# Attention and soft MoE on one core: the attention loop by pairs of heads instead of by heads

## The chip, the cores and the metric

The kernel runs on one core of a Trainium2 chip. The metric is the device time of one execution in microseconds (us). Before the change it took 432.06 us in the median of three runs (430.77 to 432.63).

The engines are named as in the profile: PE is TensorE (matmul; PEld its weight loads), DVE is VectorE, ACT is ScalarE, POOL is GpSimd, SP is the engine that issues nearly all DMAs.

## The reference

```python
# q, k, v: (8, 12, 448, 64); every head on its own, causal
scores = np.where(mask, -1e9, (q @ k.T) / 8)
attn = exp(scores - max(scores, -1)); attn /= attn.sum(-1) + 1e-9
x = (attn @ v) of all heads, as (3584, 768)        # 448 rows a batch, 12 heads x 64 columns
logits = x @ phi                                   # (3584, 32 slots)
d = softmax(logits over the 3584 rows)             # dispatch
slot_input = d.T @ x                               # (32, 768), 4 slots an expert
slot_out[e] = relu(slot_input[e] @ w1[e]) @ w2[e]  # 8 experts, 768 -> 1024 -> 768
out = softmax(logits over the 32 slots) @ slot_out # (3584, 768)
```

All is float32. w1 and w2 together are 50 MB, the largest input.

## The kernel before

There are 96 heads; the two heads of a pair p (48 pairs, six to a batch) share the loads and the casts. All transfers are DMAs of a pair: queries and keys q(p), k(p) of 448 KB each into three raw buffers in turn (the order is k(p), q(p), k(p+1), ...), and v with a column of ones, 260 KB, into two.

**One head i.** The scores lie transposed, keys on partitions, in one of three PSUM tiles `s` of two banks. They are made in two parts. `scores1` (lines 252 to 281, seven matmuls) adds the causal mask and rounded keys times rounded queries. `max_keys` (283 to 302) finds a maximum over groups of 32 keys on DVE (one long reduction of 128x1024, two short ones); `max_row` (304 to 313) transposes them on PE (tile `rt`) and reduces them on DVE (`mr`), and `max_spread` (315 to 324) writes them into rows of `r2` on POOL. `scores2` (326 to 335, four matmuls with `k2` and `r2`) adds what the rounding left out and takes the maxima away. `exps` is one ACT instruction over the tile; it frees the tile and leaves `pt`. `attv` (341 to 353) multiplies by v with 64 output columns at a time: stationary `pt`, moving 65 columns of v (the 65th is the sum), into the PSUM bank `po`. The 448 queries are four chunks, three of 128 and a last one of 64; chunk qc needs qc + 1 products for each 64 queries. `norm` (355 to 372) divides on DVE and writes `x`.

**Operands of a pair.** On ACT `cast_k` and `cast_q` round keys and queries (`ks`, `qd`), `copy_k2` fills `k2`; on POOL `sub_k` and `sub_q` form the rests (`ks` and `r2`). `ks`, `qd` and `r2` have two buffers, `k2` one. A raw buffer is free once its subtraction is done.

**Routing.** `xtrans` (377 to 383) transposes a pair's x on PE (tile `xt`, copied by ACT to `xts`). Three times a batch `next_logits` multiplies two pairs by phi (tile `g`, 32 output columns at a time); `logits_b`, `logits_d` and `logits_e` keep a running maximum and exponentials over the rows, and `dispatch` adds d.T @ x in two halves (tile `sp`, 32 output columns). `rt`, `xt`, `g`, `sp` and `tp` (of `logits_e`) share one PSUM bank, `misc`, with one buffer.

**The order.** Every engine keeps the order in which the program is written (`keep_in_program_order`). The loop of lines 525 to 582 goes by heads, and two lists (lines 48 to 53) give the order inside an even and an odd head; `plan` and `plan_a` (448 to 460) add routing at fixed heads.

```python
("ck", "mr0", "mr1", "sp", "sk", "c3", "c0", "k3", "c12", "k1", "k0", "k2", "t0", "t2", "t1", "t3", "exp", "pa",
 "x0", "plan", "x1", "x2", "cq", "a0", "a1", "a2", "a3", "n0", "n1", "n2", "ld"),
```

Here `c`, `k` are parts of scores1 of head i+2, `t` of scores2 of head i, `exp` its exp, `x` max_keys of i+2, `mr`, `sp` the maxima of i+1, and `a`, `n` products and norm of head i-1. `ck`, `sk`, `cq` work on pair p+2, as do `sq` in the odd list; `c2` is copy_k2 of p+1. On PE a head is thus: rt, scores1, scores2, xt or routing, products with v.

**After attention** the last head's rest of the path, then the experts and the output, for which w1 and w2 stream in; 23 of their 768 KB units are loaded during attention, one in every odd pair, and 12 buffers lie where attention's tiles were.

Of the kernel before, what the change touches and what calls it, by code (L numbers as in the profile page):

```python
# [9 lines left out]
F32 = mybir.dt.float32  # L10
# [7 lines left out]
P = 128  # L18
# [14 lines left out]
NR, XB, XT = 2, 3, 3  # L33
# [14 lines left out]
ORDER = (  # L48
# [4 lines left out]
)  # L53

SC0, SC1, SC2, SC3 = 576, 0, 320, 512
RW, RC, RF = 96, 4, 20
CQ0 = (0, 128, 256, 384)
# [29 lines left out]
def attention_soft_moe(ctx: ExitStack, tc: tile.TileContext, qk, va, phi, w1, w2, out):  # L87
# [17 lines left out]
    qd_, kf_ = [fix.tile([P, 2, S], F32R, name="qd0")], [fix.tile([P, 2 * S + KP], F32R, name="ks0")]  # L105
    x_[1] = fix.tile([P, NCH, 3 * P], F32, name="x1")
    qd_.append(fix.tile([P, 2, S], F32R, name="qd1"))
    zero = fix.tile([P, P // 2], F32, name="zero")
    r_ = [fix.tile([P, RW], F32, name=f"r{i}") for i in range(2)]
    kf_.append(fix.tile([P, 2 * S + KP], F32R, name="ks1"))  # L110
# [3 lines left out]
    kf_.append(fix.tile([P, 2 * S + KP], F32R, name="k2"))  # L114
    *ks_, k2_ = (k[:, 0:2 * S].rearrange("p (h s)->p h s", h=2) for k in kf_)
# [84 lines left out]
    pob = ps_1.tile([P, NCH * VC], F32, name="po")  # L200
    po0 = pob.rearrange("p (a b)->p a b", b=VC)
    identb = const.tile([P, P], BF16, name="identb")

    nc.vector.memset(zero, 0.0)
    nc.vector.tensor_copy(out=identb, in_=ident)
    for i in range(NR):
        nc.gpsimd.memset(r2_[i][0:64, :, :].bitcast(F32), 0.0)
        if i == 0:
            nc.vector.memset(k2_[0:64, :, :].bitcast(F32), 1.0)
    nc.vector.memset(pob, 0.0)  # L210
    for k in kf_:
        nc.vector.memset(k[:, 2 * S:2 * S + KP].bitcast(F32), 0.0)
    for i in range(2):
        nc.vector.memset(r_[i], -3.0e38)
# [12 lines left out]

    def cast_q(p, hs=slice(0, 2)):
        if p < NPAIR:
            nc.scalar.activation(out=qd_[p % NR][:, hs], in_=st["raw", 0, p][:, hs], func=AF.Copy)  # L230

    def cast_k(p, hs=slice(0, 2)):
        if p < NPAIR:
            nc.scalar.activation(out=ks_[p % NR][:, hs], in_=st["raw", 1, p][:, hs], func=AF.Copy)

    def sub_k(p, hs=slice(0, 2), eng=None):
        if p < NPAIR:
            ks = ks_[p % NR][64:P, hs]
            (eng or nc.gpsimd).tensor_tensor(out=ks, in0=st["raw", 1, p][64:P, hs], in1=ks, op=ALU.subtract)

    def copy_k2(p, hs=slice(0, 2)):
        if p < NPAIR:
            nc.scalar.activation(out=k2_[64:P, hs], in_=ks_[p % NR][0:64, hs],
                                 func=AF.Copy)
# [7 lines left out]
    def scores1(i, part):  # L252
# [3 lines left out]
        ks, qd = kf_[p % NR], qd_[p % NR]  # L256
# [69 lines left out]
    def scores2(i, cs):  # L326
# [4 lines left out]
        k2, r2 = kf_[NR], r2_[p % NR]  # L331
# [9 lines left out]
    def attv(i, qcs):  # L341
        if not 0 <= i < NHD:
            return
        p, h = divmod(i, 2)
        pt, v, po = pt_[i % 2], va_[p % 2], st.get(("po", i), po0)
        begun = st.setdefault(("begun", i, id(po)), set())
        for qc in qcs:
            for c in range(qc + 1):
                col = SCOL[c] + P * (qc - c)
                for u in range(0, P if qc < 3 or i == NHD - 1 and c == 3 else 64, AW):  # L350
                    nc.tensor.matmul(po[u:u + AW, qc], pt[:, col + u:col + u + AW], v[:, c, h],
                                     start=u not in begun, stop=c == qc, skip_group_check=True)
                    begun.add(u)

    def norm(i, k):
        if not 0 <= i < NHD:
            return
        p, h = divmod(i, 2)
        if k == 0:
            if i % 6 == 0:  # L360
                xn = x_[p // 3 % XB]
                st["xn", p // 3] = xn
                for k in range(3):
                    st["x", p + k] = xn[:, :, P * k:P * k + P]
            sm = st["sm", i] = moe.tile([P, NCH], F32, tag="sm", name=f"sm{i}", bufs=2)
            nc.vector.tensor_scalar(out=sm, in0=st.get(("po", i), po0)[:, :, HD], scalar1=EPS, scalar2=None, op0=ALU.add)
        elif k == 1:
            nc.vector.reciprocal(out=st["sm", i], in_=st["sm", i])
        else:
            sm = st.pop(("sm", i))  # L370
            nc.vector.tensor_tensor(out=st["x", p][:, :, HD * h:HD * h + HD], in0=st.get(("po", i), po0)[:, :, 0:HD],
                                    in1=sm.unsqueeze(2).to_broadcast([P, NCH, HD]), op=ALU.mult)

# [74 lines left out]
    plan, plan_a = {}, {}  # L448
    for b in range(NB):
        o, last = 12 * b, b == NB - 1  # L450
        for j in range(PPB if not last else PPB - 2):
            plan_a[o + 2 * j + 4] = lambda p=b * PPB + j: xtrans(p)
        for j, r in ((0, 9), (2, 11)):
            plan[o + r] = lambda b=b, j=j: next_logits(b, j, misc(f"g{b}_{j}"))
        if not last:
            plan[o + 15] = lambda b=b: (next_logits(b, 4, misc(f"g{b}_4")), logits_b(b, lt))
            plan_a[o + 17] = lambda b=b: logits_e(b)
            hs = ((19, (0,)), (25, (1,))) if b < NB - 2 else ((19, (0, 1)),)
            for r, hfs in hs:
                plan[o + r] = lambda b=b, hfs=hfs: [dispatch(b, hf) for hf in hfs]  # L460


    warm(START[0], a=zero.bitcast(BF16))
# [26 lines left out]
    scores1_all(2)  # L490
    warm(START[3])
# [4 lines left out]
    sub_q(1, h0)  # L496
# [27 lines left out]
    nload = 0  # L524
    for i in range(NHD):
        p, h = divmod(i, 2)
        if h:
            load_qk(p + 3, 1)
            if p + 1 < NPAIR - 1:
                loads_v(p + 1)  # L530
            load_qk(p + 3, 0)
            if p % 2 and nload < RES:
                load_w(nload)
                nload += 1
        if i == NHD - 3:

            loads_v(NPAIR - 1, nc.scalar)
        if i < 2:
            scores2(i, (1, 0, 2))
            if i:  # L540
                scores1_all(3)
            scores2(i, (3,))
            exps(i)
            if i == 0:
                max_row(1, 0)
                warm(START[4], pob[:, 0:P])
                max_row(1, 1)
                sub_k(1, h1, nc.vector)
                max_spread(1)
                sub_q(1, h1)  # L550

        for n in ORDER[h]:
            if i < 2 and (n == "exp" or n[0] in "kt" or n in ("c0", "c3", "c12")):
                continue
            if i == 0 and n in ("mr0", "mr1", "sp"):
                continue
            if n[0] == "k" or n in ("c0", "c3", "c12"):
                scores1(i + 2, n)
            elif n[0] == "t":
                scores2(i, (int(n[1]),))  # L560
            elif n[0] == "a":
# [336 lines left out]
```

## Time and profile before

| | |
|---|---|
| median of the runs | 432.06 us |
| profiled execution | 430.89 us, span 429.2 us |
| mean granted TensorE clock | 0.979 |
| busy: PE, PEld | 396.0, 317.6 us |
| busy: DVE, ACT, POOL | 297.6, 287.5, 266.2 us |
| DMA | 119.18 MB, mean 278 GB/s |

The page of the profile lists groups of equal instructions as line, engine, operation, out<-in and shape, with busy time, mean ns of one, and the idle time before them and what ended most of it. All instructions carry line L71, that of the helper that keeps the order, so one goes by tiles. For PE, "128*64" means 128 rows and 64 columns of the array. A matmul's end is modelled in the trace; the distance from start to start tells more. PE's instructions are twice the matmuls where the operands are plain float32: each of those is run in two. The timeline gives start, duration, engine, operation and tiles; consecutive equal instructions are merged into one row with their count.

### The profile page before, as it was taken

What the parts mean: (1) busy time and instruction counts of PE and PEld (TensorE: products, weight loads), DVE (VectorE), ACT (ScalarE), POOL (GpSimd) and SP (SyncE); (2) the same over time, 40 slices, a digit from 0 to 9 for tenths busy, and PEclk for the clock granted to TensorE, in tenths of its full rate; (3) what the DMA queues carried; (4) which work ended last, traced back from release to release, by engine and by line L of the source; (5) the groups of instructions that cost most, each with busy time, mean ns of one, the idle gap of its engine ahead of it and who ended that gap; (6) DMA issues with size and microseconds to landing.
All of it is one profiled execution on the core that took longest, in us unless ns stands there. A gap on an engine that the chain in (4) does not pass through costs nothing. (4 is left out here: it accounts for less than half of the span.)

```text
span 429.2 us, 14091 instructions
## 1 busy us (share of the span) xinstructions
PE 396.0 (92%) x5782; PEld 317.6 (74%) x5782; DVE 297.6 (69%) x861; ACT 287.5 (67%) x400; POOL 266.2 (62%) x216
## 2 busy tenths in 40 slices
PE   6898999999999999999999999999989998998740
PEld 3687888898898889888988888898868654544430
DVE  4687788778777877787787877778775477423440
ACT  5587879787887888887878788878865211333330
POOL 5799998888888788887887888888861000000000
PEclk8999999999999999999999999999999999999985
DMA  7476777777677776777776776677759999999997
GB/s 266 137 246 225 216 267 258 248 250 224 222 260 256 238 237 213 246 254 243 237 229 226 256 269 236 211 227 268 268 210 344 411 413 422 425 419 411 400 393 328
DMA packets 34481, 119.18 MB, mean 278 GB/s; under 512 B 3824, under 2 KB 8944, under 8 KB 32880
## 3 DMA queue, kind: packets, MB, share of 16 engines
q1 hardware_dynamic: 34272, 118.01, 77.5%
q8 instruction: 46, 0.75, 0.7%
q10 hardware_dynamic: 144, 0.27, 0.2%
q14 instruction: 19, 0.16, 0.1%
HBM read 107.25 MB, written 11.01 MB: 276 GB/s over the span
## 5 line engine op out<-in xcount | busy, mean ns | idle before, releaser
L71 ACT ACTIVATE pt<-s 128x1024 f32<-128x1024 f32 x96 | 98.2, 1023 | 57.2 <-PE s L71 51.8
L71 PEld LDWEIGHTS po<-va,pt 128*64 128x64 f32 x3040 | 117.8, 137 | 22.1 <-issue 21.6
L71 PE MATMUL po<-va,pt 128*64 128x65 f32 x3040 | 131.0, 225 | 0.0
L71 DVE TRANSPOSE_TENSOR_REDUCE r<-s 128x32 f32<-128x1024 f32 x96 | 118.2, 1231 | 2.4 <-PE s L71 2.0
L71 POOL TENSOR_TENSOR r<-qk,qd 64x896 fp32r<-64x896 f32 (+1 forms) x50 | 101.2, 2023 | 6.5 <-ACT qd L71 2.7
L71 POOL TENSOR_TENSOR ks<-qk,ks 64x896 fp32r<-64x896 f32 (+1 forms) x47 | 97.8, 2080 | 6.6 <-ACT ks L71 3.5
L71 POOL TENSOR_SCALAR_AFFINE_SELECT r<-mr 14x448 fp32r<-14x448 f32 x96 | 61.9, 645 | 47.5 <-DVE mr L71 43.4
L71 PE MATMUL s<-qd,ks 128*128 128x448 f32 (+3 forms) x384 | 76.5, 310 | 2.3 <-DVE ks L71 2.3
L71 PE MATMUL s<-r,k 128*128 128x320 f32 (+3 forms) x384 | 65.0, 290 | 3.5 <-ACT k L71 2.1
L71 PEld LDWEIGHTS s<-r,k 128*128 128x128 f32 (+1 forms) x384 | 54.3, 176 | 8.3 <-POOL r L71 5.6
L71 PEld LDWEIGHTS s<-qd,ks 128*128 128x128 f32 (+1 forms) x384 | 55.3, 182 | 3.1 <-DVE ks L71 2.5
L71 DVE TENSOR_SCALAR sm<-po 128x4 f32<-128x4 f32 x95 | 15.4, 162 | 52.9 <-PE po L71 51.8
L71 ACT ACTIVATE ks<-qk 128x896 fp32r<-128x896 f32 (+1 forms) x50 | 46.1, 923 | 8.1 <-DMA qk<-in_qk_dram 4.3
L71 ACT ACTIVATE qd<-qk 128x896 fp32r<-128x896 f32 (+1 forms) x50 | 46.1, 923 | 1.8 <-DMA qk<-in_qk_dram 1.7
L71 ACT ACTIVATE k<-ks 64x896 fp32r<-64x896 f32 (+1 forms) x49 | 45.8, 934 | 1.1
L71 DVE TENSOR_TENSOR x<-po,sm 128x256 f32<-128x256 f32 x95 | 40.3, 425 | 3.3
L71 PE MATMUL s<-tri,identb 128*128 128x64 bf16 (+2 forms) x288 | 39.6, 234 | 0.0
L71 PEld LDWEIGHTS <-identb 128*128 128x128 bf16 x339 | 35.0, 107 | 4.9 <-issue 3.1
L71 DVE TENSOR_REDUCE r<-r 128x16 f32<-128x32 f32 x192 | 34.1, 177 | 5.4
L71 PE MATMUL rt<-ident,r 128*76 128x128 f32 x96 | 28.8, 300 | 2.7 <-DVE sm L71 0.8
L71 PE MATMUL xt<-ident,x 128*128 128x128 f32 x188 | 29.7, 281 | 0.1
L71 DVE TENSOR_REDUCE mr<-rt 14x32 f32<-14x128 f32 x96 | 25.8, 269 | 3.8 <-PE rt L71 3.6
(136 smaller groups left out, 360.6 us busy)
## 6 DMA issues: line engine op xcount, KB each, us to landing
qk<-in_qk_dram SPq DMA_DIRECT2D x94, 448.0 KB, 4.0
w<-in_w_dram SPq DMA_DIRECT2D x43, 768.0 KB, 6.9
w<-in_w_dram SPq DMA_DIRECT2D x10, 1536.0 KB, 19.1
va<-in_va_dram SPq DMA_DIRECT2D x47, 260.0 KB, 3.2
out_dram<-ot SPq DMA_DIRECT2D x16, 384.0 KB, 6.7
out_dram<-ot SPq DMA_DIRECT2D x2, 1536.0 KB, 9.3
qk<-in_qk_dram SPq DMA_DIRECT2D x4, 224.0 KB, 3.4
hw<-in_w_dram SPq DMA_DIRECT2D x1, 768.0 KB, 6.4
```

The costliest lines, as they stand in the source:

```text
L71: return self._tc.keep_in_program_order(op(*args, **kwargs))
```

## The change

The loop goes by pairs: `block(p)` with heads a = 2p and a+1 replaces the lists and the plan. On PE its order is scores2(a), scores1(a+2), scores2(a+1), xt of pair p-1, scores1(a+3), all with the full width; then the products with v of head a, rt(a+2), the products of head a+1, the last query chunks of both heads side by side (`attv3`), rt(a+3), and last the routing product, if there is one. `po` holds both heads in one bank, as seven groups of 65 columns: three chunks of each head and one that has head a's last chunk in rows 0 to 63 and head a+1's in rows 64 to 127. The products of both heads stand in the block of their exps, and norm is done once for a pair. rt takes 64 columns instead of 76. sub_q works on pair p+1 instead of p+2, cast_k on p+3 instead of p+2. The transposed x has two buffers instead of three.

```diff
-NR, XB, XT = 2, 3, 3
+NR, XB, XT = 2, 3, 2
...
-            nc.tensor.transpose(out=st["rt", i][0:RW - RF, 0:P], in_=r_[i % 2][:, RF:RW], identity=ident)
+            nc.tensor.transpose(out=st["rt", i][0:AW, 0:P], in_=r_[i % 2][:, RF:RF + AW], identity=ident)
...
+    def attv3(p):
+
+        for c in range(NCH):
+            for h in range(2):
+                col = SCOL[c] + P * (NCH - 1 - c)
+                nc.tensor.matmul(po2[AW * h:AW * h + AW, NQ - 1], pt_[h][:, col:col + AW], va_[p % 2][:, c, h],
+                                 start=False, stop=c == NCH - 1, skip_group_check=True)
...
+    def block(p):
+        a, b = 2 * p, p // 6 - 1
+        last, m6 = p == NPAIR - 1, p % 6
+        begun = set()
+        if not last and p + 1 < NPAIR - 1:
+            loads_v(p + 1)
+        elif not last:
+            loads_v(p + 1, nc.scalar)
+        if p % 2 and p // 2 < RES:
+            load_w(p // 2)
+
+        scores2(a, range(NCH))
+        exps(a)
+        scores1_all(a + 2)
+        for k in range(3):
+            max_keys(a + 2, k)
+        scores2(a + 1, range(NCH))
+        if m6 == 2 and b >= 0 and p > 6:
+            logits_e(b)
+        if p:
+            xtrans(p - 1)
+        exps(a + 1)
+        scores1_all(a + 3)
+        max_keys(a + 3, 0)
+        sub_q(p + 1)
+        load_qk(p + 3, 1)
+        sub_k(p + 2)
+        load_qk(p + 3, 0)
+        if m6 == 1 and p > 6:
+            logits_d(b, lt)
+        copy_k2(p + 1)
+        cast_q(p + 2)
+        cast_k(p + 3)
...
+        attv(a, [(qc, qc, FULL) for qc in range(3)], po2, begun)
+        max_row(a + 2, 0)
+        attv(a + 1, [(qc, 3 + qc, FULL) for qc in range(3)], po2, begun)
+        max_row(a + 2, 1)
+        max_spread(a + 2)
+        for k in (1, 2):
+            max_keys(a + 3, k)
+        attv3(p)
+        norm(p, 0)
+        max_row(a + 3, 0)
+        max_row(a + 3, 1)
+        max_spread(a + 3)
+        for _ in range(2):
+            if later and p:
+                later.pop(0)()
+
+        if m6 in (3, 5) and p > 6:
+            sp = misc(f"sp{b}_{m6 // 5}")
+            dispatch_a(b, m6 // 5, sp)
+        for k in (1, 2):
+            norm(p, k)
+        if m6 in (3, 5) and p > 6:
+            dispatch_b(b, m6 // 5, sp)
+        if m6 in (2, 4) and p >= 2:
+            next_logits(p // 6, m6 - 2, misc(f"g{p}"))
+        elif m6 == 0 and p:
+            next_logits(b, 4, misc(f"g{p}"))
+            logits_b(b, lt)
+
+    for p in range(NPAIR):
+        block(p)
...
-                     dynamic_dma_scratch_size=1024)
+                     dynamic_dma_scratch_size=256)
```

`later` holds twelve one-off fills on POOL, now two in a block. Ahead of the loop, three memsets of x's last chunks on DVE and cast_k of pair 2 on ACT are added; the warm-up matmuls and scores1 of head 2 that stood between the first heads' steps go out or into block 0. In the last block head a's products stand alone, and the last head's path behind the loop stays as it was, without the xt of pair 46.

More of the change, by code (lines that the diff above doesn't have):

```diff
@@ L349, in attv @@
                 col = SCOL[c] + P * (qc - c)
[L350 to L358, printed above, removed]
-        if k == 0:
[L360 to L366, printed above, removed]
+                for u, w in us:
+                    if u and qc == NCH - 1 and c < qc:
+                        continue
+                    nc.tensor.matmul(po[w:w + AW, k], pt[:, col + u:col + u + AW], v[:, c, h],
+                                     start=w not in begun, stop=c == qc, skip_group_check=True)
+                    begun.add(w)
@@ L446, in dispatch @@
         dispatch_b(b, hf, sp)
[L448 to L463, printed above, removed]
+    warm(START[0], a=x_[1][:, NCH - 1, 0:AW].bitcast(BF16))
     h0, h1 = slice(0, 1), slice(1, 2)
```

162 lines of the change are left out of this document (67 added, 95 removed), and 4 rows, old and new, of the table ORDER.

## The prediction

> **What bounds the kernel now.** I read the page first, then the stretches, then one pair of heads in order of time. The page's engine line and costliest groups (busy, mean ns of one, idle time before and who ended it):
>
> ```profile
> PE 396.0 (92%) x5782; PEld 317.6 (74%) x5782; DVE 297.6 (69%) x861; ACT 287.5 (67%) x400; POOL 266.2 (62%) x216
> ...
> L71 PEld LDWEIGHTS po<-va,pt 128*64 128x64 f32 x3040 | 117.8, 137 | 22.1 <-issue 21.6
> ```
>
> The stretches, cut at every twelfth transposition of maxima (rt), are six pairs of heads each, one batch; first and last of six (us; busy us and count of PE, PEld, DVE, ACT, POOL; clock, DMA share, GB/s):
>
> ```profile
> 62.46:102.23 39.77, 39.37 (x619) 34.35 (x619) 31.52 (x91) 32.85 (x43) 33.02 (x25) 1.00 0.74 246
> 261.36:301.15 39.79, 39.39 (x620) 34.37 (x618) 31.50 (x91) 32.74 (x43) 32.90 (x25) 1.00 0.72 241
> ```
>
> A pair takes 39.78/6 = 6.63 us, TensorE has work in 99% of it, at granted clock 1.00, and DVE, ACT and POOL need 5.25, 5.46 and 5.48 us. So the order of work on TensorE sets the pace, but three engines stand within 1.4 us of it. TensorE over one head:
>
> ```profile
> 203.29 0.65 PE L71 MATMUL g<-xts,phi 128*32 128x128 f32 x16
> 203.86 1.38 PE L71 MATMUL po<-va,pt 128*64 128x65 f32 x32
> 205.17 0.30 PE L71 MATMUL rt<-ident,r 128*76 128x128 f32 x1
> 205.31 0.25 PE L71 MATMUL s<-tri,identb 128*128 128x64 bf16 x2
> 205.48 0.67 PE L71 MATMUL s<-qd,ks 128*128 128x320 f32 x3
> 205.99 0.68 PE L71 MATMUL s<-r,k 128*128 128x448 f32 x4
> 206.50 0.63 PE L71 MATMUL xt<-ident,x 128*128 128x128 f32 x4
> 207.06 0.28 PE L71 MATMUL po<-va,pt 128*64 128x65 f32 x2
> ```
>
> From start to start: first scores 0.68, second scores 0.51, x's transposition 0.56, products with v 1.31, a routing product g 0.57.
>
> **What the change takes off TensorE.** Two things. First the last query chunk. These are the weight loads of po up to a cut, and of a whole group:
>
> ```profile
> 210.36 0.77 PEld L71 LDWEIGHTS po<-va,pt 128*64 128x64 f32 x23 [0.20 <-issue]
> 203.86 1.24 PEld L71 LDWEIGHTS po<-va,pt 128*64 128x64 f32 x32 [0.20 <-issue]
> ```
>
> Less the 0.14 of one load, 23 loads start within 0.63 us, 29 ns apart; the other nine take 0.47 us, 52 ns each. The code says why: 12 products (24 loads) alternate between output rows 0-63 and 64-127, the last four (8 loads) have no partner. attv3 puts head 0 and head 1 side by side, so 16 loads a pair go from 52 to 29 ns: 16 x 0.023 = 0.37 us; with the first instruction after them, to 205.17, nearer 0.43. I take 0.40.
>
> Second, changes of tile width. po's loads sat idle 22.1 us ahead of 95 groups, 0.23 each, and 1.31 - 1.24 = 0.07 on the way out. One of two such groups a pair goes: 0.30. Nothing else leaves TensorE; the 32 products (64 loads) and both score parts stay. 6.63 - 0.70 = 5.93 us a pair if nothing else decides.
>
> **What it adds there.** The routing products (g, and sp of the dispatch) now stand right behind the second rt, and all three use the one scratch bank "misc". rt must be read by DVE (mr) first. rt takes 0.30, then mr 0.27 and two hand-offs of about 0.05: TensorE stands 0.55 us in five of six pairs, 0.46 on average. In before another head's work lies between. exps(a+1) moves behind the copy of xt on ACT, costed at 0.13 us in every other pair: a block (one pair, heads a and a+1) has second, first and second scores and xt, 0.51 + 0.68 + 0.51 + 0.47 = 2.17 us; with 0.2 until xt has ended, 0.5 for its copy and 1.05 for the exp, ACT is done at 3.92, and TensorE, after 0.68 first scores, 0.09 change of width, 0.74 products and 0.11 rt, is there at 3.79. (With 0.70 + 0.46 products and a second rt such a block, without routing, is 5.1 us.) Doing nothing there bounds it at 0, a whole exp late at 1.0. Two pairs: 11.86 + 0.92 + 0.13 = 12.9 us, against 13.26 now.
>
> **Moved steps and the chain they make.** Here is the danger. In before, sub_q(p+2) ran a pair ahead and key loads were issued straight behind it, so that cast_k had about 6.3 us from issue on:
>
> ```profile
> 197.08 2.10 POOL L71 TENSOR_TENSOR r<-qk,qd 64x896 fp32r<-64x896 f32 x1
> 199.21 0.33 SPq L71 DMA_DIRECT2D qk<-in_qk_dram  x1
> 206.37 0.64 POOL L71 TENSOR_SCALAR_AFFINE_SELECT r<-mr 14x448 fp32r<-14x448 f32 x1 [0.48 <-DVE mr L71]
> 207.09 2.11 POOL L71 TENSOR_TENSOR ks<-qk,ks 64x896 fp32r<-64x896 f32 x1
> 205.47 0.95 ACT L71 ACTIVATE ks<-qk 128x896 fp32r<-128x896 f32 x1
> 203.40 1.02 ACT L71 ACTIVATE pt<-s 128x1024 f32<-128x1024 f32 x1 [0.83 <-PE s L71]
> 202.74 0.27 DVE L71 TENSOR_REDUCE mr<-rt 14x32 f32<-14x128 f32 x1
> 202.93 1.23 DVE L71 TRANSPOSE_TENSOR_REDUCE r<-s 128x32 f32<-128x1024 f32 x1
> 200.99 0.40 DVE L71 TENSOR_REDUCE r<-r 128x16 f32<-128x32 f32 x2
> ```
>
> Over the whole run ACT waited for keys five times:
>
> ```profile
> ACT ks L71 <- DMA qk<-in_qk_dram: 4.3, 5, 1.4
> ```
>
> The three raw buffers turn over so that k(p+3) takes the one of q(p+1). In after, sub_q(p+1) is emitted in block p itself, behind both spreads of block p-1 on POOL, and cast_k(p+3) ends block p on ACT, with exps of the next block queued behind it. From the end of sub_q: issue 0.03, landing L, hand-off 0.07, cast 0.95, exp 1.02, hand-off 0.07 (2.14 + L); then the first scores of the second head, whose bank that exp frees, 0.84 to their end (205.31 to 205.48 + 0.67) and 0.03 to their reduction; 1.23, mr of the head before 0.20, two reductions 0.40, hand-off 0.05, rt 0.30; mr 0.10 + 0.27, hand-off 0.07, spread 0.64 + 0.08, sub_q 2.10 (6.31). That closes over two blocks: **two pairs take at least L + 8.45 us**. In the block with logits_e the scratch bank goes rt, tp, copies on ACT, xt, before those scores: some 1.2 us more, once in three hops.
>
> L is the unknown. Every other block issues a 768 KB weight load 2.4 to 3.0 us ahead of the keys, and only those blocks matter (a load alone gives 3.3 + 8.45 = 11.75, under 12.9). The DMA view, cut to single issues: keys at 185.84, 199.21, 212.42 and 238.99 behind a weight load; keys at 192.5 with a free queue; keys 3.7 us behind a weight load at 39.08; and the weight load at 314.98, which had only va 0.4 us ahead of it:
>
> ```profile
> qk<-in_qk_dram SPq DMA_DIRECT2D x1, 448.0 KB, 5.3
> qk<-in_qk_dram SPq DMA_DIRECT2D x1, 448.0 KB, 5.7
> qk<-in_qk_dram SPq DMA_DIRECT2D x1, 448.0 KB, 5.2
> qk<-in_qk_dram SPq DMA_DIRECT2D x1, 448.0 KB, 6.0
> qk<-in_qk_dram SPq DMA_DIRECT2D x1, 448.0 KB, 3.2
> qk<-in_qk_dram SPq DMA_DIRECT2D x1, 448.0 KB, 3.4
> w<-in_w_dram SPq DMA_DIRECT2D x1, 768.0 KB, 4.4
> ```
>
> In the four slow cases q (0.4 us) and va (1.1) had been issued just ahead of the weights. In after, SP issues va, weights, then keys some 2.9 us later, and q comes over 1.4 us ahead; that is nearest to the last row, where the weights had landed by 4.4. So L lies between 3.2 and 6.0; I take 3.6, near the free queue. The hops are then 12.9, 12.9 and 12.05 + 1.2 = 13.25: 39.05 a batch, 0.73 less than 39.78. Over some 40 pairs (6.67 batches): -4.9 us.
>
> POOL's own order (two subtractions, two spreads, four hand-offs: 2.10 x 2 + 0.64 x 2 + 0.3 = 5.8) is covered under 6.4 a pair. Norm over seven columns costs DVE about what it saves, and DVE has 1.4 us a pair to hide it. Two buffers for the transposed x cost nothing: g has read pairs p-2 and p-1 before xt(p) is written, a block later. The smaller DMA scratch costs nothing, as no issue in the rows is POOL's.
>
> **Start and end.** The first spread ends at 13.50; in after block 0 can begin there and reach rt of head 3 after its 5.1 us, at 18.6 against 20.21: -1.6. The three new memsets of x's last chunks (about 0.35 each, an estimate from the 0.81 of 896 columns below) stand on DVE before 4.05, where it had waited 0.87 for ACT: 0.2 is uncovered, and 1.05 if that cover goes. At the end, the row at 326.18 is the last rt and that at 331.75 the last head's products; the last row is the stretch of the first seven pairs:
>
> ```profile
> 12.86 0.64 POOL L71 TENSOR_SCALAR_AFFINE_SELECT r<-mr 14x448 fp32r<-14x448 f32 x1 [2.76 <-DVE r L71]
> 20.21 0.28 PE L71 MATMUL rt<-ident,r 128*76 128x128 f32 x1 [0.81 <-DVE sm L71]
> 326.18 0.30 PE L71 MATMUL rt<-ident,r 128*76 128x128 f32 x1
> 331.75 1.25 PEld L71 LDWEIGHTS e<-va,pt 128*64 128x64 f32 x34
> 333.86 0.60 PE L71 MATMUL xt<-ident,x 128*128 128x128 f32 x4
> 1.76 0.81 DVE L71 MEMSET k<- 64x896 f32 x1
> 4.05 0.62 DVE L71 TENSOR_TENSOR ks<-qk,ks 64x448 fp32r<-64x448 f32 x1 [0.87 <-ACT ks L71]
> 17.81:62.46 44.65, 42.01 (x663) 37.34 (x662) 34.70 (x97) 35.62 (x41) 41.92 (x41) 1.00 0.67 225
> ```
>
> After has one head less outstanding (rt + 1.2 of g + 3.7 = 4.9 against 5.6) and no xt in between: -1.3. The first seven pairs run at 6.38 us with POOL busy 94%, its one-off fills included; I expect 6.2 there: -1.2. The weight stream behind starts when attention frees its memory, so it moves along one for one. Sum: -4.9 - 1.6 - 1.3 - 1.2 = -9.0. The profiled execution took 430.89 (span 429.2), the median is 432.06; I count from the median: **423 us**.
>
> **Rivals.** (1) *The keys come late, slower.* If the queue behaves as in the four slow rows, L is 5.0 (half a microsecond off for the emptier queue): hops 13.45, 13.45, 14.65 = 41.55, +1.77 a batch, +11.8; the first seven pairs lose 7 x (6.73 - 6.38) = 2.4, start and end give 2.9: 443. At L = 5.5 a batch is 43.05: some 455. It decides from L about 4.5 on, where a batch takes 40.05 and the first pairs and that loss take back what start and end give. For it: four rows of the same distance; against: 3.4 and 4.4. (2) *TensorE's gain passes whole*, no chain, no bank wait: 5.93 a pair, 47 x 0.70 = -33: 399. It needs L below 3.4 and mr ready at once; ACT and POOL would then have work in 92% of a pair (5.46 and 5.48 of 5.93), which leaves little room for waits in their order. (3) *rt doesn't fit into the narrow stage*: it shrinks to 64 columns to stay there. If a transposition still takes the whole array, the group is left and entered twice more, 2 x 0.30 a pair: each hop 1.2 longer, 14.1, 14.1, 14.45, +2.9 a batch, +19, less 4 at start and end: 447. The trace has only full-width ones (128*76). The Trainium skill, "TensorEngine Tiling (Array Packing)", Restrictions and Gotchas, says that column tiling and transpose mode exclude each other for fp32 inputs; by that rule this rival holds. No run here shows it yet. (4) *Nothing to tell*: L near 4.5 eats the gain: 432.
>
> **How the numbers follow.** A measurement here tells no change to about 0.5%, 2.2 us. Forecast 0.48 (its own range 413 to 429), late keys 0.25, whole gain 0.08, wide rt 0.07, no difference 0.12. Faster: 0.48 + 0.08, less 0.02 that falls near the bound: 0.54; same 0.15; slower 0.31. The range leaves out the whole gain and the worst late keys: 410 to 445.
>
> **What would show it.** Right: loads of po 29 ns apart to the end of the group, half as many idle entries; ACT ks waiting for DMA qk in every other pair; g and sp of TensorE waiting for DVE mr. Wrong: no DMA wait ahead of ks (no chain, rival 2), or landings over 4.5 us in the blocks with weights (rival 1), or a gap on both sides of each rt (rival 3).

## The result, and the profile after

The changed kernel takes **451.7 us** in the median of four runs (449.92 to 452.62); the kernel before took 431.41 beside it (430.72 to 432.63). The ratio is 1.0462, with a 95% interval of 1.0419 to 1.0505: slower by 4.6%, where 423 us had been forecast, and outside the range of 410 to 445.

The page of the kernel after (engine line, chain by engine, loads of po):

```profile
PE 389.0 (86%) x5763; PEld 297.2 (66%) x5763; DVE 300.0 (67%) x817; ACT 288.5 (64%) x400; POOL 264.3 (59%) x215
...
PE 48%; DMA 20%; DVE 9%; issue 7%; POOL 6%; ACT 6%; SPq 0%; DVEq 0%; POOLq 0%; ACTq 0%
...
L65 PEld LDWEIGHTS po<-va,pt 128*64 128x64 f32 x3040 | 97.9, 139 | 17.9 <-issue 11.9
```

TensorE does work in 7 us less, in a span that is 20.7 us longer: it waits now, in 14% of the span instead of 8%. The loads of po save 20 us of busy time against 117.8 before, and their idle time with the releaser "issue" is down from 21.6 us in 89 places to 11.9 in 48, so the side-by-side stage and about half as many entries are there.

Stretches of the kernel after: the first seven pairs, then two of the six batches of twelve rt (us; busy and count of PE, PEld, DVE, ACT, POOL; clock, DMA share, GB/s), and the sum of all six:

```profile
15.73:64.75 49.02, 42.55 (x696) 35.99 (x693) 35.98 (x97) 36.47 (x43) 41.48 (x41) 1.00 0.68 220
...
143.25:187.55 44.30, 40.14 (x623) 33.23 (x619) 31.92 (x85) 32.84 (x43) 32.70 (x24) 0.96 0.68 216
...
230.63:272.11 41.48, 38.63 (x622) 31.90 (x619) 31.85 (x85) 32.61 (x43) 32.72 (x24) 1.00 0.70 227
...
sum 255.05, PE 233.75 PEld 192.68 DVE 191.14 ACT 197.65 POOL 196.53; mean PE 38.96 PEld 32.11 DVE 31.86 ACT 32.94 POOL 32.75
```

Six batches took 6 x 39.8 before; now they take 255.05. The quietest takes 41.48, so +1.7 a batch (10 us) is there always; the others add 6 us in all.

Where the 20.7 us of span are, from the starts of rt: up to rt of head 2 **-2.1** (15.73 against 17.81); the seven pairs behind it **+4.4** (49.02 against 44.65); from there to the last rt **+13.7** (277.4 against 263.7: six batches counted from that rt take 255.05 against 238.69, +16.4, and the pairs behind them 22.4 against 25.0, -2.7, since one of these took 8.9 before); from the last rt (342.18, before 326.18) to the end **+4.7** (107.7 against 103.0).

One pair with a g and without any late transfer takes 6.80 us instead of 6.50. First its stretch before and after, then TensorE over it in the kernel after:

```profile
205.17:211.67 6.50, 6.50 (x110) 5.84 (x109) 5.02 (x15) 5.28 (x7) 5.49 (x5) 1.00 0.58 178
```

```profile
201.84:208.64 6.80, 6.35 (x112) 5.40 (x108) 5.17 (x14) 5.27 (x7) 5.45 (x4) 1.00 0.82 277
```

```profile
201.84 0.30 PE L65 MATMUL rt<-ident,r 128*64 128x128 f32 x1
202.58 0.64 PE L65 MATMUL g<-xts,phi 128*32 128x128 f32 x16 [0.45 <-DVE mr L65]
203.15 0.74 PE L65 MATMUL s<-r,k 128*128 128x448 f32 x4
203.73 0.26 PE L65 MATMUL s<-tri,identb 128*128 128x128 bf16 x2
...
204.49 0.63 PE L65 MATMUL s<-r,k 128*128 128x448 f32 x4
204.96 0.63 PE L65 MATMUL xt<-ident,x 128*128 128x128 f32 x4
205.43 0.25 PE L65 MATMUL s<-tri,identb 128*128 128x128 bf16 x2
...
206.25 0.92 PE L65 MATMUL po<-va,pt 128*64 128x65 f32 x24
207.10 0.30 PE L65 MATMUL rt<-ident,r 128*64 128x128 f32 x1
207.33 1.39 PE L65 MATMUL po<-va,pt 128*64 128x65 f32 x40
208.64 0.30 PE L65 MATMUL rt<-ident,r 128*64 128x128 f32 x1
```

```profile
207.32 1.25 PEld L65 LDWEIGHTS po<-va,pt 128*64 128x64 f32 x40
```

From start to start, in us:

| part of a pair | before | after |
|---|---|---|
| products with v, with the rt of the first head | 1.31 + 0.14 + 1.31 = 2.76 | 0.85 + 0.23 + 1.31 = 2.39 |
| second rt up to the next instruction | 0.14 | 0.74 |
| first and second scores, xt | 3.03 | 3.10 |
| g | 0.57 | 0.57 |

The 40 loads of 207.32 stand 28 ns apart (1.25 less the 0.14 of one, over 39): side by side works to the end of the group. But of the 0.70 us that were to go only 0.37 went, and 0.60 came in at the scratch bank. That is +0.30 for a pair whose TensorE meets nothing else.

The waits of the kernel after (us in total, times, longest) that bear on this:

```profile
ACT ks L65 <- DMA qk<-in_qk_dram: 19.2, 20, 2.4
PEld g L65 <- DVE mr L65: 14.6, 23, 0.6
```

ACT's waits for keys went from five to twenty, 4.3 to 19.2 us, as the chain of the forecast says; but they are the smaller part of the loss. The landings that the forecast called the unknown: keys issued behind a weight load, from 63.39 to 318.16, took 3.2 to 6.0 us, 4.3 in the median, where 3.6 was taken. The four slowest of them (5.3 to 6.0) stand ahead of pairs of 7.6 to 9.7 us.

### The profile page after: what moved, and what is told of

Read it like the earlier page. It is cut to its first block, busy times and chain, and to the rows that moved or that the text cites. A ratio compares the mean times of both kernels' runs of the same rounds, so it can differ in the third digit from the quotient of the medians.

```text
span 449.9 us, 14022 instructions
## 1 busy us (share of the span) xinstructions
PE 389.0 (86%) x5763; PEld 297.2 (66%) x5763; DVE 300.0 (67%) x817; ACT 288.5 (64%) x400; POOL 264.3 (59%) x215
## 4 chain that ended last, share of the span: by engine, by line
PE 48%; DMA 20%; DVE 9%; issue 7%; POOL 6%; ACT 6%; SPq 0%; DVEq 0%; POOLq 0%; ACTq 0%
PE s L65 17%; PE po L65 16%; DMA w<-in_w_dram 14%; DMA qk<-in_qk_dram 7%; POOL r L65 5%; DVE r L65 4%; PE xt L65 4%; PE rt L65 3%; ACT pt L65 3%; PE sp L65 2%; PE g L65 2%; DVE mr L65 2%; PE pp L65 1%; PE hp L65 1%; POOL ks L65 1%
## 5 line engine op out<-in xcount | busy, mean ns | idle before, releaser
L65 PE MATMUL po<-va,pt 128*64 128x65 f32 x3040 | 111.1, 226 | 0.1
L65 PEld LDWEIGHTS po<-va,pt 128*64 128x64 f32 x3040 | 97.9, 139 | 17.9 <-issue 11.9
L65 PE MATMUL s<-qd,ks 128*66 128x64 f32 (+3 forms) x384 | 78.4, 315 | 2.6 <-DVE ks L65 1.9
L65 PEld LDWEIGHTS s<-r,k 128*128 128x128 f32 (+1 forms) x384 | 59.1, 175 | 20.4 <-POOL r L65 13.3
L65 PE MATMUL s<-r,k 128*128 128x448 f32 (+3 forms) x384 | 65.8, 294 | 3.6 <-POOL r L65 3.6
L65 ACT ACTIVATE ks<-qk 128x896 fp32r<-128x896 f32 (+1 forms) x50 | 45.6, 914 | 21.5 <-DMA qk<-in_qk_dram 19.2
L65 PEld LDWEIGHTS s<-qd,ks 128*128 128x128 f32 (+1 forms) x384 | 49.8, 181 | 4.0 <-DVE ks L65 2.4
L65 ACT ACTIVATE xts<-xt 128x512 f32<-128x512 f32 x47 | 28.0, 597 | 29.2 <-PE xt L65 29.2
L65 PE MATMUL s<-tri,identb 128*128 128x128 bf16 (+2 forms) x288 | 43.2, 235 | 3.2 <-ACT pt L65 3.2
L65 PEld LDWEIGHTS <-identb 128*128 128x128 bf16 x320 | 27.2, 99 | 7.1 <-issue 5.3
L65 DVE TENSOR_TENSOR x<-po,sm 128x384 f32<-128x384 f32 (+2 forms) x49 | 26.7, 547 | 7.4 <-PE sp L65 6.0
L65 DVE TENSOR_SCALAR sm<-po 128x7 f32<-128x7 f32 (+1 forms) x48 | 7.9, 165 | 31.6 <-PE po L65 31.6
```

The lines of the kernel that those rows point to most:

```text
L65: return self._tc.keep_in_program_order(op(*args, **kwargs))
```

## The experiments

Theories. **K**: the keys come late, and the chain key, cast, exp, scores, maxima, subtraction paces the pairs (rival 1). **W**: rt breaks the narrow stage (rival 3). **B**: the scratch bank holds TensorE behind the second rt. **D**: DVE's order, the norm of a pair in one lump, holds the next rt. **T**: the stream of weights starts late at the end. The ratios are to the kernel before on the same chip, with their 95% intervals.

**late_cast.** Keys cast a block later, so that no landing is in the chain (the cast of pair 2 ahead of the loop goes too):

```diff
         exps(a)
+        cast_k(p + 2)
         scores1_all(a + 2)
@@
-        cast_k(p + 3)
```

> The changed kernel with one step moved: cast_k(p+2) stands behind the first exp of block p instead of cast_k(p+3) at the end of block p, so that no exp waits behind keys that are still on their way. Theory K (the chain of keys is what costs): its waits for DMA on ACT (19.2 us in 20 waits) go, and most of the loss of 20 us with them: 432 to 437 us. Theory W (TensorE's own order costs: the narrow stage is broken by rt, and routing waits for the scratch bank): only the few long blocks of 7.5 to 9.7 us shrink to 6.8 to 7.2, 444 to 448 us.

Measured: 450.05 us, 1.0465 (1.0431 to 1.0498), above the figures of both theories. ACT's waits for keys fell to 4.9 us, and the batches (one of them, and the sum of six):

```profile
102.64:144.30 41.66, 38.75 (x623) 31.90 (x619) 31.82 (x85) 32.29 (x43) 32.90 (x25) 1.00 0.71 230
...
sum 251.17, PE 232.47 PEld 191.37 DVE 190.99 ACT 193.35 POOL 197.54; mean PE 38.75 PEld 31.90 DVE 31.83 ACT 32.22 POOL 32.92
```

With few late keys four of the six batches take 41.65, still 1.85 more than before, and the ratio is the same. K costs some 4 us in six batches (255.05 less 251.17); it isn't the main cause. That the time hardly moves has a second reason: the first seven pairs take 50.71 instead of 49.02, and two of them 9.97 and 9.10 instead of 7.99 and 7.66.

**rt76.** rt takes 76 columns again: `in_=r_[i % 2][:, RF:RW]`, and 76 rows of the output.

> The changed kernel with rt over 76 columns again, as before the change, which cannot go in a 64-column tile. If a transposition of 64 columns takes the whole array anyway (theory W), nothing changes: within 0.5% of the changed kernel, 450 to 453 us, and the same 150 ns ahead of rt and 230 ns behind it. If the narrow form saves two changes of width a pair, this one loses 2 x 0.30 us in 47 pairs: 475 to 480 us.

Measured: 449.99 us, 1.0459 (1.0423 to 1.0496), pairs of 6.8 and 7.0 to 7.2 as in the kernel after. The narrower rt brings nothing: at 64 columns, too, it stands 0.23 us from start to start before the next product, and the first product behind it is no earlier.

**mid2.** Both rt side by side in one tile of the scratch bank, between the products of the second head and the last chunks:

```diff
...
-        max_row(a + 2, 0)
         attv(a + 1, [(qc, 3 + qc, FULL) for qc in range(3)], po2, begun)
-        max_row(a + 2, 1)
-        max_spread(a + 2)
         for k in (1, 2):
             max_keys(a + 3, k)
+        max_row(a + 2, 0)
+        max_row(a + 3, 0)
+        for i in (a + 2, a + 3):
+            max_row(i, 1)
+            max_spread(i)
         attv3(p)
         norm(p, 0)
-        max_row(a + 3, 0)
-        max_row(a + 3, 1)
-        max_spread(a + 3)
```

> The changed kernel with both rt side by side, in two column ranges of one scratch tile, between the products of head a+1 and the last chunks; their maxima are read before the routing products begin. Theory W: TensorE's wait of 0.45 to 0.65 us ahead of g and sp goes in five of six pairs, some 0.45 a pair: 20 us less, 430 to 434 us. Theory K: the key chain holds the pace, no more than 4 us less: 448 us or more.

Measured: 451.24 us, 1.0487 (1.0452 to 1.0522). In the batches the bank's wait is gone: pairs with a g fall from 6.81 to 6.60, and six batches take 249.31 instead of 255.05. The time stays because the first seven pairs take 52.95 instead of 49.02, with three of 7.8 to 10.1 us, and because the pair with logits_e still takes 7.4 to 8.4. TensorE's loads wait for POOL 48 times, 24.4 us (13.3 in the kernel after); the longest of these waits, 1.9 to 2.5 us, stand in the first seven pairs. So the time lies in K's branch, but not through the keys. The six batches:

```profile
69.51:318.82 249.31, 235.44 (x3712) 193.30 (x3709) 197.26 (x511) 198.25 (x253) 194.93 (x145) 1.00 0.72 231
```

**side and side_fix.** The kernel before, loop by heads, with only the last chunks side by side (a third `pt`, the norm of a pair behind its second head). side leaves out the first half of the dispatch of every batch but the last, and both halves for the last but one, so it does less than the reference; side_fix does all of it, with the first half of each dispatch one head earlier, and divides each head's columns behind that head. Both also take the small DMA scratch and the two buffers for the transposed x from the change.

```diff
+        pair = p < NPAIR - 1
...
+        if pair and 3 in qcs:
+            if h:
+                for c in range(NCH):
+                    for g in range(2):
+                        col = SCOL[c] + P * (NCH - 1 - c)
+                        nc.tensor.matmul(po2[AW * g:AW * g + AW, NQ - 1], pt_[(2 * p + g) % NPT][:, col:col + AW],
+                                         v[:, c, g], start=False, stop=c == NCH - 1, skip_group_check=True)
+            return
```

> The kernel before with one part of the change alone: the loop by heads stays, but the last query chunks of both heads go side by side into one bank, with one norm a pair; for room a third pt buffer, two buffers for the transposed x, the first routing product of a batch two heads earlier. If TensorE's order sets the pace there and the gain passes: 47 x 0.46 us (16 loads at 58 ns become 29 ns) = 21 us less than before, 408 to 412 us. If the order of ACT or POOL takes part of it (each has work in 82 to 83% of a pair): 415 to 422 us. If the side-by-side form itself doesn't give what the rows say: 428 us or more.

> The kernel before, loop by heads, with only the last chunks side by side, as in side, but with nothing left out (the first half of each dispatch comes one head earlier) and with the norm in two parts, each behind its own head. If side lost because of the lump of the norm on DVE, a pair falls from 7.11 to 6.63 - 0.4 = 6.2 to 6.5, and the time to 411 to 425. If it lost because the loop by heads itself can't use the shorter products (a wait on DVE or the scratch bank in each head takes their place), it stays at 430 or more.

Measured: side 451.14 us, 1.0479 (1.0427 to 1.0530); side_fix 456.13 us, 1.0599 (1.0553 to 1.0645). Both lie in the slowest branch of their forecast: with the shorter products alone the loop by heads is slower too, though the products themselves are as short as hoped (in side a head with 40 loads takes 1.32 us up to its rt). In side_fix, from 214.52 to 221.12, a pair without routing products takes 6.60 (the shortest pair before, one with tp, takes 6.16); the stretch, TensorE and the wait over the run:

```profile
214.52:221.12 6.60, 5.53 (x96) 5.00 (x92) 5.37 (x16) 5.27 (x7) 5.29 (x5) 1.00 0.60 194
...
217.93 0.28 PE L72 MATMUL rt<-ident,r 128*76 128x128 f32 x1 [1.07 <-DVE sm L72]
...
PE rt L72 <- DVE sm L72: 30.6, 47, 1.3
```

TensorE's work there is 5.53 us, but behind the odd head DVE has sums, reciprocal, two parts of x (0.36 and two of 64x64, 0.57), mr and the long reduction before the even head's rt, and the even head has 24 loads to cover it, not 32. What is saved on TensorE is handed to a wait for DVE, 30.6 us in all. Another 9.7 us of side_fix's loss are the earlier dispatch's own: seven times sp stands right behind xt and waits for ACT's copy, in pairs of 8.9 us. The tail is 103.6 and 103.8, as before: T belongs to the loop by pairs.

**rt_wide.** The first rt ahead of all products:

```diff
-        attv(a, [(qc, qc, FULL) for qc in range(3)], po2, begun)
         max_row(a + 2, 0)
+        attv(a, [(qc, qc, FULL) for qc in range(3)], po2, begun)
```

> The changed kernel with the first rt of a pair (head a+2) moved ahead of all products with v, behind the first scores of head a+3, so that the narrow stage (24 + 40 products) is no longer broken by it; everything else stays. If the break costs what the rows of the kernel after show (152 ns ahead of rt and 229 + 101 behind it, against 58 each, so some 0.31 us a pair), a pair falls from 7.09 to about 6.8 us, 47 pairs give -14, and the time is about 437. If the pace is set elsewhere (POOL's or DVE's chain of maxima, keys), the break's time turns into another wait and the time stays at 448 to 452. Theory of the bank wait: no change from this edit, since both rt still share the bank with g and sp.

**g_late.** The routing one stage later:

```diff
         scores2(a, range(NCH))
+        if m6 == 2 and b >= 0 and p > 6:
+            logits_e(b)                     # was ahead of xtrans(p - 1)
         exps(a)
+        routing(p - 1)                      # next_logits, second half's dispatch; were behind max_spread(a + 3)
```

> The changed kernel with the routing products (g, sp of the second half) and the two transpositions of logits_e moved one stage on: from right behind the second rt, respectively from ahead of xt, to behind the first head's second scores of the next pair; only sp of the first half stays behind rt, as x is overwritten there. The scratch bank is then read by DVE while other work runs. If TensorE's waits at the bank are what makes pairs long (g and sp 0.45 to 0.64 in five of six pairs, xt 1.2 to 1.4 in one of six, about 3 us a batch once one sp keeps its wait), a pair falls by 0.5 us to about 6.6 and the time to about 427. If pairs are paced by the chain keys - cast - exp - scores - maxima, or by the order of work on DVE and POOL, less than a third of it comes: above 442.

**both** is the two together, **both_late** adds late_cast's edit and puts `norm` behind `max_spread(a + 3)`.

> rt_wide and g_late together. If break and bank are two separate costs on TensorE, their gains add: 7.09 - 0.31 - 0.5 = 6.28 us a pair, 47 pairs give -38, about 412, below the kernel before. If another engine or the key chain (two pairs at least L + 8.45, so 6.0 to 7.2 a pair for landings of 3.6 to 6.0) takes over, it stops at 6.6 to 6.8 a pair, 427 to 437, with ACT ks waiting for DMA qk longer than in the kernel after.

> both, and also the cast of keys of pair p+2 right behind the first exp of pair p (in place of that of p+3 at the end of the block), which takes landings out of the chain, and mr of head a+3 ahead of the norm on DVE. If keys and the lump of the norm on DVE are what is next after break and bank, this is faster than both by 1 to 10 us, at about 405 to 412; if not, it is the same as both within 2 us.

Measured: rt_wide 451.39 us, 1.0471 (1.0432 to 1.0510); g_late 444.18, 1.0322 (1.0283 to 1.0361); both 443.23, 1.0272 (1.0223 to 1.0322); both_late 440.76, 1.0234 (1.0194 to 1.0274). rt_wide and g_late lie in their second branch, where another order sets the pace, and both and both_late are some 30 us above the 412 and 405 to 412 of their first; both_late isn't clear of both. Each edit takes its cost off TensorE; the time follows only in part. In both_late the stage with v is whole, 229.61 to 231.83, 2.22 us with its rt: the break costs 2.39 - 2.22 = **0.17 us** a pair by these rows (the way in from the scores lies outside the 2.39). In g_late an undisturbed pair with a g takes 6.21, 0.59 less, so the bank costs what the table says. The stretches (g_late, then rt_wide) and what waits instead (g_late's keys; rt_wide's first rt):

```profile
211.10:217.31 6.21, 6.21 (x112) 5.34 (x108) 5.17 (x15) 5.16 (x7) 4.48 (x5) 1.00 0.80 249
...
ACT ks L65 <- DMA qk<-in_qk_dram: 29.4, 26, 2.0
```

```profile
200.50:207.39 6.89, 6.25 (x112) 5.33 (x109) 5.15 (x14) 5.50 (x7) 5.45 (x4) 1.00 0.89 290
...
PEld rt L65 <- ACT xts L65: 19.4, 44, 0.5
...
PE rt L65 <- DVE r L65: 7.3, 35, 0.6
```

g_late's other pairs stay long: ACT waits for keys 29.4 us in place of 19.2, which points to K behind B. In rt_wide rt stands where it needs xt's copy and r earlier than these are there. both_late shows D in the clear (TensorE, then DVE in the same pair):

```profile
229.61 0.27 PE L65 MATMUL rt<-ident,r 128*64 128x128 f32 x1 [0.79 <-DVE r L65]
229.81 2.08 PE L65 MATMUL po<-va,pt 128*64 128x65 f32 x64
231.83 0.30 PE L65 MATMUL rt<-ident,r 128*64 128x128 f32 x1
```

```profile
225.32 0.28 DVE L65 TENSOR_REDUCE mr<-rt 14x32 f32<-14x128 f32 x1 [1.16 <-PE rt L65]
...
226.41 0.57 DVE L65 TENSOR_SCALAR x<-po,sm 64x64 f32<-64x64 f32 x2
227.02 0.29 DVE L65 TENSOR_TENSOR lt<-g,lt 128x128 f32<-128x128 f32 x1
...
227.79 1.24 DVE L65 TRANSPOSE_TENSOR_REDUCE r<-s 128x32 f32<-128x1024 f32 x1
```

DVE waits 1.16 us for the second rt and then has mr, the norm, the routing's additions and the reduction in one row, up to 229.03, and two short reductions behind it; rt waits for these. Over the run rt waits so for r 33 times, 10.7 us, and for xt's copy 9 times, 4.0 us.

**split.** both_late with the first head's columns divided right behind mr of head a+2. Here the norm writes part of x before the first half's dispatch has read it, so that sum is another one; the work is the same.

> both_late with the norm on DVE in two parts: the first head's three columns right behind mr of head a+2, where DVE stood idle 1.1 us for rt, the second head's three and the last chunks behind mr of head a+3. In both_late TensorE waits 0.2 to 0.8 us for r ahead of the first rt, since DVE has mr, the whole norm (1.46 us), the routing's addition (0.3 to 0.8) and the long reduction (1.24 + 0.4) in one row between the end of the products and that rt. If this row on DVE is what paces a pair, it falls by some 0.5 us, a pair from 6.77 to 6.2-6.35 and the time from 440.8 to 416-424. If the products of the last chunks, which now wait for the first part's read of their bank, or POOL and ACT (5.5 us of work each) take over, a pair stays above 6.6 and the time at 433 or more.

Measured: 482.0 us, 1.1194 (1.1143 to 1.1246): its second branch and the wait named there, but some 49 us above that branch's bound. The row that counts:

```profile
PEld po L65 <- DVE x L65: 47.2, 47, 1.0
```

The last chunks write the bank that DVE reads, and the program makes them wait for the end of that read, 0.9 to 1.0 us in each pair. A norm in parts needs a second bank; that was not tried.

**early_disp.** The last but one batch's second half of the dispatch one block earlier:

```diff
         exps(a)
+        if p == NPAIR - 2:
+            dispatch(NB - 2, 1)             # was in the last block, behind attv(a)
```

> The changed kernel with one half of a dispatch moved: the second half for the last batch but one, which the change put into the last block behind the products of head 94, is done a block earlier, behind the second scores of head 92; nothing else. In the kernel after, SP stands from 339.47 to 347.61 at a load of weights whose buffer lies over x, which that dispatch reads last (sp ends at 347.55), and eight further loads are issued right behind it. If this holds the weights back, the load goes out by about 342 to 344, the tail from the last rt falls from 107.8 to 103-105 and the time to about 446. If the loads wait for the last scores or products instead, or the tail is set by TensorE's own work, the tail stays at 107 to 108 and the time at 450.

Measured: 447.12 us, 1.0396 (1.0336 to 1.0456). The tail falls from 107.7 to 102.1. TensorE and SP's issues of weights in the kernel after, then SP in early_disp:

```profile
346.70 0.85 PE L65 MATMUL sp<-x,gs 128*32 128x384 f32 x8
...
331.82 7.61 SPq L65 DMA_DIRECT2D w<-in_w_dram  x3
...
347.61 2.06 SPq L65 DMA_DIRECT2D w<-in_w_dram  x4
```

```profile
336.57 2.49 SPq L65 DMA_DIRECT2D w<-in_w_dram  x3
...
342.51 0.33 SPq L65 DMA_DIRECT2D w<-in_w_dram  x1
```

In the kernel after, SP issues nothing from 339.43 (331.82 + 7.61) until sp has read x at 347.55, and then the next weights within a few microseconds; in early_disp they go out from 342.51 on. T is shown by the tail. The edit costs 3.6 us of its own, in a pair of 10.7 us: two sp follow each other on the scratch bank, the second waits 1.2 us for DVE, and TensorE's clock is low behind that stop (last section).

**best, best2, after_sid.** best is g_late, late_cast and early_disp (behind the first scores of head 94, where the bank is free), with mr ahead of the norm, the first half's addition ahead of the norm and one instead of two one-off fills of POOL in a pair. The first rt stays between the products, where DVE has time for r. best2 is best, and after_sid the kernel after, with this:

```diff
-    later += ...                            # memset sid, four sid_part, copy srep: two in each early pair
@@ behind the last block
+    nc.gpsimd.memset(sid, 0.0)
+    for g in range(4):
+        sid_part(g)
+    nc.gpsimd.tensor_copy(out=srep, ...)
```

> Built from what the runs so far point to: g_late (routing products one stage later; the first rt stays between the products of the two heads, where DVE has time for r) with late_cast's cast of keys, early_disp's earlier last dispatch (here behind the first scores of head 94, so that the bank is free by then), mr ahead of the norm on DVE, the addition of the first half's dispatch ahead of the norm, and one instead of two of POOL's one-off fills a pair. Undisturbed pairs in g_late are 6.22 us with a g, some 6.6 with sp, 6.5 with logits_e and 7.0 with the sp that keeps its wait: 38.8 a batch against 39.8 in the kernel before, -6.5 in 6.67 batches; the tail is to be 102 to 103 as in the kernel before. If the stalls found (bank wait, late keys, held weights) are all there is, the time is 420 to 428, below the kernel before. If DVE's or POOL's order brings new waits as in both_late, it is 430 to 437.

> best with six one-off jobs of POOL (the fills of sid and the copy srep, which only the tail reads) moved from the first pairs to behind the last spread. In best the pairs 8 to 11 take 8.2, 7.6, 7.7 and 7.7 us in place of 6.3 to 7.0, with TensorE waiting 1.1 to 1.5 us for POOL's spread (s <- POOL r): there each spread stands on POOL behind a subtraction of 2.1 us, while in later pairs both spreads come ahead of both subtractions. If the fills bring this, some 4.5 us go: 425 to 427, and no pair from 2 to 12 above 7.1 us. If POOL's work as such (5.5 of 6.3 us) is the cause there, the time stays at 430.

> The changed kernel with only that edit: the six jobs moved behind the last spread. In the kernel after, the pairs 5 to 7 take 7.4, 8.0 and 7.7 us in place of some 6.9. If the fills bring these too, 2 to 3 us go, about 447.5; if late keys do, it stays at 450.

Measured: best 430.23 us, 0.9993 (0.9970 to 1.0016); best2 **425.98 us, 0.9897 (0.9873 to 0.9920)**; after_sid 448.52, 1.0439 (1.0405 to 1.0474). best is outside its 420 to 428 and just inside the 430 to 437 of new waits, because pairs 8 to 11 take 8.2, 7.6, 7.7 and 7.7 us. POOL in best there, then in best2:

```profile
71.49 0.64 POOL L65 TENSOR_SCALAR_AFFINE_SELECT r<-mr 14x448 fp32r<-14x448 f32 x1 [0.92 <-DVE mr L65]
72.79 2.09 POOL L65 TENSOR_TENSOR r<-qk,qd 64x896 fp32r<-64x896 f32 x1 [0.66 <-ACT qd L65]
74.95 0.64 POOL L65 TENSOR_SCALAR_AFFINE_SELECT r<-mr 14x448 fp32r<-14x448 f32 x1
```

```profile
71.14 0.64 POOL L65 TENSOR_SCALAR_AFFINE_SELECT r<-mr 14x448 fp32r<-14x448 f32 x1 [0.65 <-DVE sm L65]
71.86 2.11 POOL L65 TENSOR_TENSOR r<-qk,qd 64x896 fp32r<-64x896 f32 x1
73.91 2.12 POOL L65 TENSOR_TENSOR ks<-qk,ks 64x896 fp32r<-64x896 f32 x1
```

In best a subtraction of 2.1 us comes between the two spreads of a pair, in best2 both spreads come first. So it is the order on POOL that the fills bring about, not its work. The block as written has both subtractions and then both spreads, so behind these fills POOL does not keep the order of the program; why is not shown. Without them no pair from 2 to 12 is above 7.03, from second rt to second rt, and a batch of best2 takes 39.27, 0.5 less than before:

```profile
96.68:135.95 39.27, 38.37 (x623) 31.84 (x619) 31.32 (x85) 32.74 (x43) 32.77 (x24) 1.00 0.76 243
```

best2 keeps the change's stage with v and its pairs, without these stalls, and is faster than both kernels, by 1.0% than the one before. Of its parts, mr ahead of the norm and the earlier addition were not run alone, nor were the small DMA scratch and the two buffers for the transposed x, which best2 keeps.

## Why the prediction was wrong

Of the 29.7 us between the -9.0 of the forecast and the +20.7 of the span, 18.6 are in the batches and pairs up to the last rt (-4.9 forecast, +13.7 measured), 6.0 at the end and 5.6 in the first seven pairs; the start came 0.5 better.

**The sum on TensorE.** (a) Side by side: right. (b) "One of two such groups a pair goes: 0.30" failed, for two reasons. The first rt cuts the narrow stage, 0.17 us a pair by both_late against the kernel after. And even whole, products and rt take 2.22 in place of 2.76, 0.54 and not 0.70 less; how that splits between the loads and the entry isn't settled. So 0.37 was gained where 0.70 was booked. Rival 3 had the mechanism at 0.07 and a price of 0.60. The Trainium skill, "TensorEngine Tiling (Array Packing)", Gotcha 2, lists column tiling and transpose mode as exclusive for float32. The trace agrees in so far as a 64-column rt leaves the stage (0.23 us to the next product) and rt76 costs no more than it. (c) The bank: 0.55 forecast, 0.60 measured. It was right, and enough to undo the rest: the sum of the pair's terms should have read -0.37 + 0.60 + 0.07 = +0.30, a slower kernel before any key is late. Two undisturbed pairs take 13.7 to 14.0 us in the kernel after, where 12.9 was forecast.

**The key chain.** It exists, as drawn: ACT waits for keys in 20 places. But the forecast took it for the pace (39.05 a batch) while TensorE's own order stood above it at 41.5. Taking landings out of the chain (late_cast) shortens six batches by 4 us and leaves the ratio at 1.0465. Of the rivals' figures 447 (wide rt) came near, and 443 (late keys) less so, but each for a cause that holds a part only: 0.17 us in 47 pairs is 8 us, and what the batches take beyond the quietest is 6 of the 20.7. The worst figure of the late keys, 455 at landings of 5.5, is as near as 447; the landings were 4.3 in the median. The one batch of 44.30 has a pair of 9.7 us, with logits_e: its keys landed 5.3 us after their issue, ACT waited 1.2 us for them, xt waited 1.9 us for ACT's copies of tp, and the clock was lower behind that (below).

**logits_e.** Put at 1.2 us and only in the chain of keys; on TensorE that pair went from 6.16 to 6.86 at best, as tp, ACT's copies and xt share the bank.

**DVE's norm.** "Costs DVE about what it saves" is true of its time and missed its place: a pair's norm is one row of 1.5 us where there were two of 0.8. In the kernel after, the bank's wait hides that; side_fix and both_late show it as the next limit.

**Start and end.** The start: -1.6 forecast, -2.1 measured at rt of head 2. That is mostly luck: 1.6 of it are there at rt of head 0 already (10.48 against 12.11), since in the profile before the clock over the same instructions was 0.53 from 8.5 to 11.9, and in the one after it was 1.00. The new order alone gives 0.45 from there to rt of head 2, 1.3 to rt of head 3, where the forecast counted. The first seven pairs: -1.2 forecast, +4.4 measured. I carried their gain over from the batches, whose sign was wrong; and POOL's one-off jobs went from one in each head to two in each pair of the program, with the order seen in best behind them (four sid_part in a row at 42.82, and from 43.98 to 58.70 spreads and subtractions by turns): with six of them moved away (after_sid) the pairs of 7.4, 8.0 and 7.7 us take 7.2, 6.8 and 7.1, 2 us less. The ratio of after_sid, 1.0439, is not clear of the 1.0462. The end: "the weight stream moves along one for one" failed. It moved by 5 us more, since the last dispatch of the batch before, at head 91 in the kernel before, stands in the last block now; it reads x, on whose memory weights are to land, and SP issues in order. The step I worked out for each queue of the loop I did not work out for the last block's SP.

## What to carry to other kernels

When a stage is regrouped so that one engine switches less often, list what stands between the regrouped instructions and which buffer it shares: an operation that stays in the middle keeps the switch, and a single scratch bank used twice in a row costs a whole round trip. A reordering of a loop also moves the last reader of each tile; follow the queue that waits for that memory to the end of the kernel. And a shorter TensorE stage was worth nothing here until the work of the engine that it covered had been placed elsewhere: taken away alone, late keys, the bank's wait, the held weights and POOL's fills brought the ratio from 1.046 to 1.046, 1.032, 1.040 and 1.044 (of these only 1.032 is clear of 1.046 by its interval), and all of them, with DVE's order, to 0.990.

## What the hardware showed that was not expected

A short stop of TensorE can be followed by about half its clock. In early_disp it is idle from 335.2 to 336.4, and the granted clock of the next 3.6 us is 0.53; in the kernel after, the same behind the slow pair's stop:

```profile
335.20:336.40 1.20, 0.05 (x2) 0.00 (x0) 1.07 (x3) 1.02 (x1) 1.20 (x1) 1.00 0.04 14
336.40:340.00 3.60, 3.54 (x18) 2.25 (x19) 1.13 (x2) 0.00 (x0) 0.14 (x1) 0.53 0.70 216
```

```profile
153.20:154.50 1.30, 0.00 (x0) 0.00 (x0) 0.40 (x3) 1.30 (x5) 1.30 (x2) 1.00 0.03 11
155.00:159.00 4.00, 4.00 (x60) 3.39 (x60) 1.80 (x4) 3.73 (x5) 1.32 (x2) 0.63 0.62 213
```

The Trainium skill, "TensorE: Matmul & The Clock Gate", Part 1, puts the drop behind an idle window of about 3.4 us. Here stops of 1.2 and some 1.9 us were followed by it, and the time at the low clock was 3 to 4 us. Not every such stop was: in the kernel after, one as long left the clock at 1.00:

```profile
53.35:55.22 1.87, 0.00 (x1) 0.01 (x1) 1.78 (x4) 1.09 (x2) 1.74 (x2) 1.00 0.37 121
55.22:59.22 4.00, 4.00 (x76) 3.53 (x77) 1.87 (x5) 2.71 (x4) 2.62 (x2) 1.00 0.54 150
```

In early_disp so did a stop of 1.44 us, from 195.50 to 196.94. What decides between the two isn't shown. The shorter waits of 0.45 us in each pair left the clock at 1.00.
